# Later copies of the MLP's sums and a re-ordered head in a fused top-32 attention and MLP kernel

## The chip, the cores and the metric

The kernel runs on one core of a Trainium2 chip. The metric is the device time of one execution in microseconds, the median of several runs. Engines are called by their short names in the profile: PE (TensorE, matmuls; PEld its weight loads), DVE (VectorE), ACT (ScalarE), POOL (GpSimd) and SP (SyncE, which issues the DMAs).

## The reference

```python
scores = 1/sqrt(D) * q @ k^T                    # 8 batches, 8 heads, S=576, D=64
kth    = 32nd largest score of each row
attn   = softmax of the scores that are >= kth  # the others count as nothing
x      = (attn @ v), heads side by side         # 4608 x 512
h      = x @ w_in                               # 512 x 2048
g      = h where h >= 1, 0 where h <= -1, else (h + 1)^2 / 4
out    = g @ w_out                              # 2048 x 512
```

The two weight matrices arrive as 64-bit floats, which the kernel converts itself.

## The kernel before

**Work.** The attention is cut into 144 steps, called m: for each batch four tiles of 128 rows, each with four pairs of heads, and two more steps for the last 64 rows of each head. Each step goes through the engines:

- `scores` (L349): PE multiplies into `sp` (L367), ACT copies it to `s` (L368, two copies);
- the 32nd largest value on DVE: `more` and `less` are the larger and smaller of two halves of a row (L381, made for the step to come), then rounds of MAX8 and MATCH_REPLACE (L384 to L455) and a scan (L460);
- on ACT the negative maximum `nmax` (L402, it needs DVE's first `tops`, L401) and the exponentials `e` (L404);
- on DVE the masked sum (L467), which needs `e` and the 32nd value;
- division by the sum (`divide`, L411): in the head ACT makes a diagonal matrix `diag` (L417) and the division falls to the transpose on PE; later POOL divides (L420);
- the transpose of the weights: in the head by PE (`transpose_w` L476: `pw` L482, copies L485 and L489), later by DMA (`move_w` L493: ACT splits into `halves` L497, a DMA writes `rows`, a transposing DMA reads them into `wT`);
- `values` (L506): PE multiplies with v into `po` (L514, L522), ACT copies to `xT` (L527, L529).

When all four head pairs of a 128-row tile are done, `mlp` (L538) makes its work pending. There are 36 such chunks. A chunk has eight *hidden* blocks of 8 matmuls (PE, `ph`, L547), *reads* of each of them on ACT (`r` L558, `g` L566), *bounds* on POOL (L573, L575, L576) and 16 *final* matmuls into one PSUM tile `py` (L586). The profile counts each of these matmuls twice: 4608 for `ph` (36 x 64 x 2), so 16 a block and 32 finals a chunk. After the last of these ACT copies `py` into `y` (L589) and SP sends `y` out (L591). `py` has a single buffer, so the first final matmul of the next chunk waits for the copy. The last chunk is finished in halves (L600, L612).

**The head.** While the weights are converted (32 pieces of 512 words, `convert_piece` L141: `units` on ACT L147 and L148, `bits` on DVE L156, the addition on POOL L158), the steps m = 0 to 7 are *early*: four pieces a step, transposes by PE, one step of scores begun per step (slot 4). Step 8 is called `first_late` in the code: the first step after the last piece. Keys of the first batch are transposed by PE into `pk` and `pkt` (L261, L269) and copied to `kT` (L265, L274).

**What sets the order.** Every engine's order is written out by hand: all instructions are issued inside `manual_schedule`, in the order of the loop L801 to L890. A step has seven slots. In each slot the loop puts a part of the top-32 search, loads, transposes, values, scores and key preparation at fixed places; at its end `advance` hands out pending MLP work by a budget (`due`, a share of the work left), and `take` pops one item. `holding` keeps the reads of hidden blocks back in some slots, and `bounds` are delayed by two slots in late steps.

**Lines that the change touches.** `load_keys`/`keys_of` (copy engine at L264), `final` (L579 to L591), the start of the program (L779 to L785), the slot loop (L849 to L890). `LAG` is the number of hidden blocks that run ahead of the final matmuls.

Of the kernel before, what the change touches and what calls it, by code (L numbers as in the profile page):

```python
# [26 lines left out]
def kernel(  # L27
# [149 lines left out]
    def run(ctx, paired):  # L177
# [61 lines left out]
        def keys_of(b):  # L239

            kT = stage.tile([P, NHP, S], F32, name="kT")
            k_tl = stage.tile([TL, H, D], F32, name="k_tl", bufs=1)
            got = dict(kT=kT)

            def load_keys(hp):
                if b == 0:
                    k_in = xtp.tile([P, NK, P], F32, name="xT").rearrange("p c (j d) -> p c j d", j=2)
                else:
                    k_in = stage.tile([P, NT, 2, D], F32, name="k_in", bufs=1)
                for j in range(2):  # L250
                    nc.sync.dma_start(out=k_in[:, :, j, :], in_=whole(k, b)[:, 2 * hp + j])
                return k_in

            k_in = load_keys(0)
            nc.sync.dma_start(out=k_tl, in_=k[b, :, SM:S, :].rearrange("h p d -> p h d"))
            yield got
            for hp in range(NHP):
                k_next = load_keys(hp + 1) if hp + 1 < NHP and b == 0 else None
                pt = ps.tile([P, NT, P], F32, name="pk", tag="a", bufs=2)
                for c in range(NT):  # L260
                    nc.tensor.transpose(pt[:, c, :], k_in[:, c].rearrange("p j d -> p (j d)"), ident)  # L261
                for j in range(2):
                    d = slice(j * D, (j + 1) * D)
                    copy = nc.vector.tensor_copy if b == 0 and hp < 2 and j else nc.scalar.copy  # L264
                    copy(kT[d, hp, main(j)], pt[d].rearrange("p c n -> p (c n)"))  # L265
                if hp == 0:
                    pt = ps.tile([P, NHP, TL], F32, name="pkt", tag="a", bufs=2)
                    for h2 in range(NHP):
                        nc.tensor.transpose(pt[:, h2, :], k_tl[:, 2 * h2:2 * h2 + 2].rearrange("p j d -> p (j d)"),  # L269
                                            ident[0:TL, 0:TL])  # L270
                    for j in range(2):
                        d = slice(j * D, (j + 1) * D)
                        copy = nc.vector.tensor_copy if b == 0 and j else nc.scalar.copy
                        copy(kT[d, :, tail(j)], pt[d])  # L274
                k_in = load_keys(hp + 1) if hp + 1 < NHP and b else k_next
                if hp == NHP - 2:
                    loads = load_values(b)
                    got["v"], got["v_tl"] = next(loads)
                    for _ in loads:
                        pass  # L280
                yield got
# [256 lines left out]
        def mlp(xT, rows, pool, last):  # L538
# [39 lines left out]

            def final(f):  # L579
                if f == 0:  # L580
                    py.append(ps.tile([P, DM], F32, name="py", tag="py", bufs=1))
                if f // group not in gs:
                    issue_reads()
                while f // group not in whole_g:
                    bounds.popleft()[1]()
                nc.tensor.matmul(py[0], gs[f // group][:, f % group], w_out[:, f, :], start=(f == 0), stop=(f == NF - 1))  # L586
                if f == NF - 1:
                    y = (late or words).tile([P, DM], F32, name="y", bufs=1)
                    nc.scalar.activation(y, py[0], AF.Copy, scale=unit)  # L589
                    for p0, p1, dst in rows:  # L590
                        nc.sync.dma_start(out=dst, in_=y[p0:p1])  # L591

# [60 lines left out]
        total, spent = len(chunks) * (NK * NF + NF * DM // P), 0  # L655
        converted, inspected, due = 0, 0, 0.0

        reads, bounds, holding, slots_done = [], deque(), False, 0

        def issue_reads():  # L660
            while reads:
# [4 lines left out]
        def convert(time):  # L666

            nonlocal converted, begun
            while begun < min(converted + (2 if paired else 1), n_pieces):
                pipe.append(convert_piece(words, begun, not paired))  # L670
                next(pipe[-1])
                begun += 1
            next(pipe.popleft())
            converted += 1
            usable[converted] = time
            for i in range(begun, converted + (len(room) or 2)):
                load(words, i)
# [13 lines left out]
        def take():  # L691

            nonlocal spent, due, pe_time, taken
            cost, pieces, work, _ = pending[0]
            if pieces > converted or usable[pieces] > pe_time + 0.5:
                return False
            pending.popleft()
            due -= cost
            spent += cost
            pe_time += cost * UNIT_TIME  # L700
            work()
            taken = work.func
            return True
# [54 lines left out]
        def begin_at(m):  # L758
            nonlocal pe_time
            if m < n:  # L760
                queries(m)
                begin(m)
                pe_time += 1.15
                scored[m] = pe_time + 2.0
# [11 lines left out]
        issue(loads)  # L776
        convert(12.0)
        begin_at(0)
        convert(13.0)  # L779
        for _ in first_top(state[0]):  # L780
            pass
        begin_rest(state[0])
        for i in range(2):
            replace(state[0], 8, i)
        next(first)  # L785
        begin_at(1)
        next_keys, valued = 1, 0

        def values_until(m):
            nonlocal valued, pe_time  # L790
            while valued < min(m, n):
                pe_time = max(pe_time, ready_at[valued]) + 1.25
                values(state[valued])
                state[valued] = None
                if valued in ready:
                    ch = ready[valued]
                    mlp(xTs[ch], rows_of(*chunks[ch]), mlp_pool, ch == len(chunks) - 1)
                valued += 1

        first_late = None  # L800
        for m in range(n + 2):  # L801
# [3 lines left out]
            elif not early and late is None:  # L805
                conversion.close()
                room.clear()
                late = ctx.enter_context(tc.tile_pool(name="late", bufs=1))

            share, left = (total - spent) / (n + 2 - m), sum(x[0] for x in pending)  # L810
            for r in sorted(ready):
                if r + 4 > m and r >= valued:
# [11 lines left out]
            for slot in range(SLOTS):  # L824
# [24 lines left out]
                    judge(ps, att)  # L849
                if slot == 2 and (early or m == first_late or m >= n - 1):  # L850
                    values_until(m)
                if m == 0 and slot in (1, 2):
                    next(first)
                holding = not early and m % 2 == 0 and slot in (1, 2) and m < n
                if slot == 2 and not early:
                    if m % 2 == 0:
                        while len(reads) < 3 and pending and taken is not None and taken.__name__ == "hidden" and take():
                            pass
                    begin_until(min(m + 2, len(state)))
                    holding = False  # L860
                    issue_reads()
                    values_until((m - 2) // 2 * 2)
                    begin_until(m + 3 - m % 2)
                if slot == 4 and early:
                    begin_at(m + 2)
                if slot == (6 if early else 1):
                    queries(m + (3 if early else 5))
                    if (m < n and prep is None and next_keys < B and steps[m][0] == next_keys - 1 and steps[m][1] >= 1
                            and (next_keys > 1 or converted == n_pieces)):
                        prep = (turned_keys_of if next_keys > 1 else keys_of)(next_keys)  # L870
                    if prep is not None and (m % 2 == 0 or next_keys == 1):
                        got = next(prep, None)
                        pe_time += 0.5 if next_keys < 2 else 0.0
                        if got is None:
                            prep, next_keys = None, next_keys + 1
                        else:
                            keys[next_keys] = got
                            value_loads = got.get("loads", value_loads)
                    elif value_loads is not None:
                        loads.append(partial(next, value_loads, None))  # L880
# [3 lines left out]
                        nc.tensor.transpose(rest[:, i % NT, :], ident, ident)  # L884
                advance((EARLY_SHARE if early else share) / SLOTS if m < n - 2 else 32.0, now)
                slots_done += 1
                while bounds and (early or m >= n or bounds[0][0] < slots_done - 2):
                    bounds.popleft()[1]()
            for _ in (top_k if top_k is not None else ()):
                pass  # L890
        while pending:
            advance(32.0, pe_time + 8.0)
            while bounds:
                bounds.popleft()[1]()
        order.__exit__(None, None, None)


# [45 lines left out]
```

## Time and profile before

| what | value |
|---|---|
| median of 3 runs | 1471.31 us (1469.75 to 1472.52) |
| the profiled execution | 1471.88 us, of which the span is 1470.1 us |
| granted clock of PE in it, mean | 0.992 |
| busy: PE / DVE / ACT / POOL | 1433.2 / 1395.7 / 1160.2 / 930.9 us |
| DVE's waits for `s` (L381) | 8.8 us in 6 |
| DVE's waits for kT (L265) | 9.4 us in 2, one of them 8.0 at the start |
| PE's waits for `y` (L586) | 1.6 us in 1 |
| PE's waits for `wT` from the DMA (L514) | 4.1 us in 2 |

A line of the timeline reads: start and length in us, engine, line of the code, operation, what is written from what with shapes, how many instructions, and in brackets the idle time before it with the instruction that ended it. Lines of one kind that follow each other are put together (x2). A row of the table of stretches gives, for each engine, busy us and in brackets its instructions, then PE's granted clock (1.00 is full), the DMA engines' mean busy share and GB/s. All times are counted from the start of the span.

The kernel falls in two stages: the head with its conversion, up to about 150 us with its consequences to about 200 us, and a long regular middle in which a chunk takes 37.77 us (for example from the `y` at 1062.15 to that at 1099.92). The end after 1405 us is the rest of the last chunks' MLP.

### The profile page before, as it was taken

What the parts mean: (1) busy time and instruction counts of PE and PEld (TensorE: products, weight loads), DVE (VectorE), ACT (ScalarE), POOL (GpSimd) and SP (SyncE); (2) the same over time, 40 slices, a digit from 0 to 9 for tenths busy, and PEclk for the clock granted to TensorE, in tenths of its full rate; (3) what the DMA queues carried; (4) which work ended last, traced back from release to release, by engine and by line L of the source; (5) the groups of instructions that cost most, each with busy time, mean ns of one, the idle gap of its engine ahead of it and who ended that gap; (6) DMA issues with size and microseconds to landing.
All of it is one profiled execution on the core that took longest, in us unless ns stands there. A gap on an engine that the chain in (4) does not pass through costs nothing.

```text
span 1470.1 us, 32068 instructions
## 1 busy us (share of the span) xinstructions
PE 1433.2 (97%) x10787; PEld 1049.5 (71%) x10787; DVE 1395.7 (95%) x4392; ACT 1160.2 (79%) x2222; POOL 930.9 (63%) x1310
## 2 busy tenths in 40 slices
PE   6998899999999999999999999999999999999998
PEld 5776577777777777777777777777777777777777
DVE  6989999999999999999999999999999999999922
ACT  6986878888778888887778887888778888777642
POOL 3564577667666666666666666666666666666640
PEclk7999999999999999999999999999999999999999
DMA  7642766876778877886667797997667987665410
GB/s 233 199 133 57 201 161 183 217 188 165 164 177 211 217 200 192 210 218 177 173 168 204 207 216 177 224 215 181 174 165 187 224 214 175 167 163 151 137 41 17
DMA packets 508159, 260.42 MB, mean 177 GB/s; under 512 B 458704, under 2 KB 467152, under 8 KB 507984
## 3 DMA queue, kind: packets, MB, share of 16 engines
q1 hardware_dynamic: 507984, 258.27, 68.3%
q8 instruction: 87, 1.43, 0.4%
q14 instruction: 88, 0.72, 0.2%
HBM read 62.39 MB, written 102.63 MB: 112 GB/s over the span
## 4 chain that ended last, share of the span: by engine, by line
PE 91%; ACT 4%; DMA 2%; issue 1%; DVE 1%; SPq 1%; ACTq 0%
PE ph L547 34%; PE py L586 32%; PE sp L367 11%; PE po L514 10%; PE po L522 1%; PE pw L482 1%; DMA wT<-rows 1%; PE py_half L600 1%; ACT s L368 1%; ACT units L147 1%; ACT halves L497 1%; ACT wT L485 1%; ACT e L404 0%; DMA xT<-in_k_dram 0%; PE rest L884 0%
## 5 line engine op out<-in xcount | busy, mean ns | idle before, releaser
L547 PEld LDWEIGHTS ph<-xT,w_in 128*128 128x128 f32 x4608 | 547.0, 192 | 97.7 <-issue 66.8
L547 PE MATMUL ph<-xT,w_in 128*128 128x128 f32 x4608 | 555.6, 276 | 2.4 <-ACT g L566 1.8
L586 PE MATMUL py<-w_out,g 128*128 128x512 f32 x1120 | 526.6, 597 | 1.6 <-ACT y L589 1.6
L573 POOL TENSOR_SCALAR r<-r 128x256 f32<-128x256 f32 x280 | 138.3, 494 | 402.1 <-ACT r L558 397.9
L388 DVE MATCH_REPLACE8 more<-tops,more 128x288 f32<-128x288 f32 x864 | 379.1, 445 | 0.0
L420 POOL TENSOR_SCALAR e<-e,rz 128x576 f32<-128x576 f32 x268 | 304.3, 1145 | 12.6 <-DVE rz L413 12.6
L586 PEld LDWEIGHTS py<-w_out,g 128*128 128x128 f32 x1120 | 193.9, 191 | 164.9 <-issue 162.9
L497 ACT COPY halves<-e 128x1152 uint16<-128x1152 uint16 x268 | 293.8, 1144 | 0.0
L576 POOL TENSOR_TENSOR g<-r,g 128x256 f32<-128x256 f32 x280 | 233.4, 834 | 22.0
L467 DVE SCALAR_TENSOR_TENSOR e<-s,kth,e 128x577 f32<-128x577 f32 x288 | 242.9, 881 | 0.1
L404 ACT ACTIVATE e<-s,nmax 128x576 f32<-128x576 f32 x288 | 223.0, 775 | 4.7
L558 ACT ACTIVATE r<-ph,half 128x256 f32<-128x256 f32 (+1 forms) x296 | 136.9, 462 | 105.1 <-PE ph L547 100.5
L368 ACT ACTIVATE s<-sp 128x576 f32<-128x576 f32 x288 | 171.8, 650 | 43.2 <-PE sp L367 41.5
L575 POOL TENSOR_TENSOR r<-r 128x256 f32<-128x256 f32 x276 | 181.0, 656 | 23.0
L367 PE MATMUL sp<-kT,qT 64*128 64x288 f32 x1024 | 161.9, 434 | 4.8 <-ACT kT L265 3.4
L367 PEld LDWEIGHTS sp<-kT,qT 64*128 64x128 f32 x1024 | 89.8, 188 | 75.9 <-issue 30.5
L514 PE MATMUL po<-wT,v_in 128*64 128x128 f32 x2048 | 138.7, 276 | 4.9 <-DMA wT<-rows 4.1
L381 DVE TENSOR_TENSOR more<-s 128x576 f32<-128x576 f32 x144 | 134.7, 935 | 8.8 <-ACT s L368 8.8
L514 PEld LDWEIGHTS po<-wT,v_in 128*64 128x64 f32 x2048 | 113.4, 137 | 29.1 <-issue 12.2
L566 ACT ACTIVATE g<-ph,minus 128x256 f32<-128x256 f32 x280 | 130.8, 467 | 0.0
L429 DVE MAX8 tops<-more 128x8 f32<-128x288 f32 x288 | 125.9, 447 | 0.0
L437 DVE MAX8 tops<-more 128x8 f32<-128x288 f32 x288 | 117.0, 449 | 0.0
(95 smaller groups left out, 1370.1 us busy)
## 6 DMA issues: line engine op xcount, KB each, us to landing
rows<-halves SPq DMA_DIRECT2D x134, 576.0 KB, 3.2
lines<-parts SPq DMA_DIRECT2D x48, 256.0 KB, 3.3
q_in<-in_q_dram SPq DMA_DIRECT2D x32, 256.0 KB, 4.5
v_in<-in_v_dram SPq DMA_DIRECT2D x32, 256.0 KB, 4.0
raw<-in_moe_w_in_dram SPq DMA_DIRECT2D x32, 256.0 KB, 3.3
raw<-in_moe_w_out_dram SPq DMA_DIRECT2D x32, 256.0 KB, 3.2
out_dram<-y SPq DMA_DIRECT2D x31, 256.0 KB, 3.3
kT<-in_moe_w_in_dram SPq DMA_DIRECT2D x8, 512.0 KB, 4.5
```

The costliest lines, as they stand in the source:

```text
L367: nc.tensor.matmul(*x, start=True, stop=True)
L368: nc.scalar.activation(s[:, :, c0:c1], sp[:, :, 0:SH], AF.Copy, scale=SCALE)
L388: nc.vector.match_replace(out=st["rest"][:, i, :], in_to_replace=eight(st["tops"], i, r - 8), in_values=src[:, i, :], imm_value=LOWEST)
L404: nc.scalar.activation(e[:, i, :], s[:, i, :], AF.Exp, bias=nmax[:, i:i + 1])
L420: nc.gpsimd.tensor_scalar(st["e"][:, i, :], st["e"][:, i, :], rz[:, i:i + 1], 1.0, ALU.mult, ALU.mult)
L467: nc.vector.scalar_tensor_tensor(out=st["all"][1][:, i, :], in0=st["all"][0][:, i, :], scalar=last[i], in1=st["all"][1][:, i, :], op0=ALU. ...
L497: nc.scalar.copy(halves[:, :, i * S:(i + 1) * S], st["e"][:, i, :].bitcast(U16).rearrange("p (k t) -> p t k", t=2))
L514: nc.tensor.matmul(po[j * D:(j + 1) * D], v_in[:, h, c, :] if c < NT else tail_values(v_tl, h, t), wT[:, block(j, c)], start=(c == 0), sto ...
L547: nc.tensor.matmul(ph[:, i], w_in[:, kk, f * P:(f + 1) * P], xT[:, kk], start=(kk == 0), stop=(kk == NK - 1))
L575: nc.gpsimd.tensor_tensor(out=r, in0=r, in1=r, op=ALU.mult)
L576: nc.gpsimd.tensor_tensor(out=g, in0=r, in1=g, op=ALU.add)
L586: nc.tensor.matmul(py[0], gs[f // group][:, f % group], w_out[:, f, :], start=(f == 0), stop=(f == NF - 1))
```

## The change

Four edits; the computation is the same.

1. The copy of `py` into `y` and the output DMA are put into a queue, `outputs`. In the head (steps up to m = 8) an entry is issued more than three slots later, otherwise at the end of the slot of its last final matmul; the first final matmul of the next chunk always empties the queue first.
2. The second pair of keys is prepared right behind the first scores instead of after the first step's maxima; the second of its two copies goes from DVE to ACT.
3. Step 8 is treated like an early step for values, scores, queries and held reads: values first, then the scores of step 10, then up to `LAG` items of pending MLP work at once. The scores of step 11 and the next queries and keys come in step 9 instead.
4. The second batch's keys are prepared in odd late steps (9, 11, 13, 15) instead of in every step from 8 on; those of the later batches stay in even steps.

```diff
-                    copy = nc.vector.tensor_copy if b == 0 and hp < 2 and j else nc.scalar.copy
+                    copy = nc.vector.tensor_copy if b == 0 and hp == 0 and j else nc.scalar.copy
...
             def final(f):
                 if f == 0:
+                    while outputs:
+                        outputs.popleft()[1]()
                     py.append(ps.tile([P, DM], F32, name="py", tag="py", bufs=1))
...
                 if f == NF - 1:
-                    y = (late or words).tile([P, DM], F32, name="y", bufs=1)
-                    nc.scalar.activation(y, py[0], AF.Copy, scale=unit)
-                    for p0, p1, dst in rows:
-                        nc.sync.dma_start(out=dst, in_=y[p0:p1])
+                    outputs.append((slots_done, partial(give, py[0])))
+
+            def give(total):
+                y = (late or words).tile([P, DM], F32, name="y", bufs=1)
+                nc.scalar.activation(y, total, AF.Copy, scale=unit)
+                for p0, p1, dst in rows:
+                    nc.sync.dma_start(out=dst, in_=y[p0:p1])
...
         begin_at(0)
+        next(first)
         convert(13.0)
...
-        next(first)
         begin_at(1)
...
+            head = early or m == first_late
...
+                if slot == 2 and m == first_late:
+                    begin_at(m + 2)
+                    for _ in range(LAG):
+                        if pending:
+                            take()
...
-                holding = not early and m % 2 == 0 and slot in (1, 2) and m < n
-                if slot == 2 and not early:
+                holding = not head and m % 2 == 0 and slot in (1, 2) and m < n
+                if slot == 2 and not head:
...
-                if slot == (6 if early else 1):
-                    queries(m + (3 if early else 5))
+                if slot == (6 if head else 1):
+                    queries(m + (3 if head else 5))
...
-                    if prep is not None and (m % 2 == 0 or next_keys == 1):
+                    if prep is not None and (early or m % 2 == (1 if next_keys == 1 else 0)):
...
                 slots_done += 1
+                while outputs and (not head or outputs[0][0] < slots_done - 3):
+                    outputs.popleft()[1]()
...
             while bounds:
                 bounds.popleft()[1]()
+            while outputs:
+                outputs.popleft()[1]()
```

More of the change, by code (lines that the diff above doesn't have):

```diff
@@ L656, in run @@
         converted, inspected, due = 0, 0, 0.0
-        reads, bounds, holding, slots_done = [], deque(), False, 0
+        reads, bounds, outputs, holding, slots_done = [], deque(), deque(), False, 0
         def issue_reads():
```

## The prediction

> **What bounds the kernel now.** I read the page's engine totals first, then single stretches, because the totals mix two stages.
>
> ```profile
> PE 1433.2 (97%) x10787; PEld 1049.5 (71%) x10787; DVE 1395.7 (95%) x4392; ACT 1160.2 (79%) x2222; POOL 930.9 (63%) x1310
> ```
>
> TensorE and VectorE share the bound; ScalarE has room. The table of stretches says where (TensorE busy, weight loads, VectorE, ScalarE, GpSimd, clock, DMA share, GB/s).
>
> ```profile
> 118.00:137.00 19.00, 16.52 (x123) 1.00 0.23 62
> 137.00:165.00 28.00, 21.19 (x155) 0.94 0.61 175
> 165.00:196.00 31.00, 29.40 (x226) 1.00 0.63 165
> 256.00:1405.00 1149.00, 1148.90 (x8681) 1.00 0.75 189
> ```
>
> These rows count TensorE alone. From 256 to 1405 it never stands still, and VectorE doesn't either: both show 50.00 in every 50 us row. So nothing can be won there, only lost. Before 196 TensorE idles 2.48 + 6.81 + 1.60 = 10.9 us. There VectorE leads, and its waits are in its timeline (start, length, and in brackets the idle time before with its releaser).
>
> ```profile
> 16.98 0.69 DVE L265 COPY kT<-pk 64x512 f32<-64x512 f32 x1 [1.37 <-ACT kT L265]
> ...
> 131.55 0.76 DVE L381 TENSOR_TENSOR more<-s 128x576 f32<-128x576 f32 x1 [2.80 <-ACT s L368]
> ```
>
> ScalarE's timeline shows the old place of the sum's copy, `y`, first in the head, then at a chunk's end late in the kernel:
>
> ```profile
> 122.40 0.60 ACT L589 ACTIVATE y<-py 128x512 f32<-128x512 f32 x1 [2.91 <-PE py L586]
> 122.89 0.68 ACT L417 ACTIVATE diag<-ident,rz 128x128 f32<-128x128 f32 x2
> ...
> 1099.92 0.60 ACT L589 ACTIVATE y<-py 128x512 f32<-128x512 f32 x1 [0.88 <-PE py L586]
> 1100.72 0.21 ACT L402 ACTIVATE nmax<-tops 128x2 f32<-128x2 f32 x1 [0.20 <-DVE tops L401]
> ...
> 1102.81 2.19 ACT L497 COPY halves<-e 128x1152 uint16<-128x1152 uint16 x2
> 1104.90 0.77 ACT L404 ACTIVATE e<-s,nmax 128x576 f32<-128x576 f32 x1
> ```
>
> And TensorE's timeline shows who needs the one `py` buffer next:
>
> ```profile
> 195.39 1.10 PE L586 MATMUL py<-w_out,g 128*128 128x512 f32 x2 [1.60 <-ACT y L589]
> ```
> ```profile
> 1105.08 1.02 PE L586 MATMUL py<-w_out,g 128*128 128x512 f32 x2
> ```
>
> At 195 the copy already stood behind `halves` (194.65, ended 195.24), and TensorE waited. At 1105 it doesn't: `y` was over at 1100.52.
>
> [...]diag waits 2.91 us behind a `y` that it doesn't need. [...]The trace shows half (0.50) in 10.6–20.8, 24.2–31.05 and 143.7–147.1[...]. [...]`more` takes 0.74 us at best and 1.13 at 1098.15, where a division of GpSimd (L420) began at 1097.93.[...]
>
> **The change part by part.**
>
> *Second keys behind the first scores; one key copy moved to ScalarE.* VectorE loses the wait of 1.37 and the copy of 0.69 in step 0: 2.1 us. It could fall short: `sp` of step 1 at 17.00 had waited 3.40 for that kT, and s(1) was ready at 20.70 for a `more` at 21.19. Both kT copies now precede the second piece's units on ScalarE, and s(1) moves forward with them. The next key load is issued one weight load earlier on SP; behind it stands that weight load, one issue later. Price 0 to 2.1; I take −2.1.
>
> *Step 8 like the head.* The order of the engines in the changed program, timed with the durations of the same instructions before: without `y` ahead of diag, pw starts at 122.36 instead of 123.34, wT ends at 124.45, po runs 125.1–126.9, sp(10) follows at once, s(10) is ready at 128.85. So `more`(10) starts at about 128.9 and its 2.80 wait goes. What is late next: four hidden blocks now follow sp(10). 48 matmul records take 5.52 (L547 at 133.03), a block has 16, so 1.84, four 7.3: 128.0 to 135.3. Their four r/g pairs, then `y` (136.05), stand on ScalarE ahead of nmax(9) and e(9). The first half of e(9) is over at about 137.55, where the masked sum of step 9 (L467), come early, stands ready at 133.3: a new wait of 4.25. Net 4.25 − 2.80 = +1.43: step 9 ends at about 139.05 instead of 137.62. Behind it s(11) is ready at 141.9 for a need at 142.25, just in time. At 196 I take +1.2 of it as left (GpSimd's divisions move too). Bounds: −2.8 (no wait for e(9)) to +2.6[...].
>
> The sum for the head is −2.1 + 1.2 = −0.9, within ±1.2. It passes to the end, since TensorE's start at 195.39 hangs on ScalarE and so on VectorE.
>
> *Second batch's keys in odd steps.* Four pairs of kT copies (1.16) and pk (0.60) at steps 9 to 15 instead of 8 to 11, first used in step 18. Cover: two steps; without it one step's scores would come late. Price 0; up to 0.5 either way, since the copies stand before other r/g pairs.
>
> *Sums copied later.* In 23 chunks, those with `y` at 456.94 to 1288.94, `y` goes from ahead of nmax to behind both `halves`. (In the seven boundaries at 195 to 424 it stood there already; the last ones keep their place.) Of 0.60 us 0.49 is its own. Putting 0.49 behind the end of `halves`, and taking off `y` ahead of nmax where nmax didn't wait for VectorE (457, 609, 646), leaves against the next `py`: five boundaries with +0.12 to +0.38, and 18 short by 0.16 to 0.40, in sum 5.44. At 1105: halves end at 1105.00, plus 0.49 is 1105.49, `py` wanted 1105.08: short by 0.41. When TensorE does wait, it starts 0.15 after `y` ends (195.24 to 195.39): 18 × 0.15 = 2.7. Together 8.2 us, if every boundary pays in full.
>
> It does if VectorE, on whose tops nmax waits, falls back with TensorE; it pays once (0.6) if VectorE keeps its own pace and so arrives earlier at the next boundary. The trace has something between: the distance of `halves` to the next `py` leaves its level of about −0.23 or −0.37 three times by 0.5 to 0.6 (608.7, 948.8, 1288.9) and is back after one or two chunks. So a lead of VectorE costs it about as much per chunk as the lead is[...]. A lead d then meets wait w − d = d: half of w is paid, **4.1 us**. Bounds 0.6 and 8.2. The output DMA moves on SP to right ahead of the transposed reads (3.3 us landing); the read of w has 2 to 6 us of slack in odd steps: 0.
>
> *GpSimd's divisions one triple later*, once a chunk from 164 to 947. Example at 832.51: the triple can start when g is written (833.62), takes 0.40 + 0.61 + 0.73, the division then 1.47 to 2.77: over at 836.8 to 838.1; `halves` needs it at 838.10. Covered, barely. Bounds: `more` regains 0.23 there (hidden, as TensorE sets the pace), or `halves` slips 0.5 in 13 of these boundaries: 6.5. I take 0.
>
> Sum: the profiled execution has 1471.88 (span 1470.1 and 1.8 around it), 0.6 over the median of 1471.31. −0.9 + 4.1 = **+3.2**: 1475.1 against the profiled run, 1474.5 against the median. I give **1474.5**, own range 1472 to 1478.6.
>
> **Rivals.**
> 1. *Paid once.* VectorE runs on, ScalarE's chain comes 0.4 earlier, the wait vanishes: −0.9 + 0.6 gives 1471.0. For it: the slack in the boundaries 233 to 424, where `y` stands behind `halves` already, wanders between 0.33 and 1.88 with no second wait. Against it: from 495 on the distance is held.
> 2. *Faster: the hand-over of step 8 to 9 keeps both gains.* Place: the masked sum L467 of step 9. Price: −2.1 − 2.8 = −4.9, so 1466.4, if boundaries cost nothing. For it: TensorE has 10.9 us of idle time before 196 and the four blocks fill some. Against: r/g stand in strict order ahead of e(9). It decides at a wait for e(9) below 1.5 us, where the four blocks would have to end near 132.5.
> 3. *Full price.* VectorE follows TensorE entirely or `halves` slips behind the division: −0.9 + 8.2 gives 1478.6, more with a slip.
> That the change does nothing is excluded: copies and `y` do move in the built order.
>
> **How the numbers follow.** A difference under 0.2% (2.9 us) can't be told from none here. Forecast 0.48 (about 0.36 beyond that bound, 0.12 within), rival 1 0.18, rival 2 0.24, rival 3 0.10. Faster 0.24, same 0.12 + 0.18 = 0.30, slower 0.36 + 0.10 = 0.46. Range 1466.0 to 1479.5: from rival 2 to just over the full price.
>
> **What would show it.** Right: no copy L265 of keys on VectorE at 17; `more`(10) without its 2.80; a wait of about 4 us of L467 for e(9) near 133; TensorE's waits listing "py L586 <- ACT y" some 18 more times, 0.2 to 0.5 each, in sum 2 to 8 us; TensorE below 50.00 per 50 us after 457. Wrong: no such waits after 457 (rival 1), or L467 without wait (rival 2), or TensorE waiting in the middle for something that I gave nothing: wT or scores.

## The result, and the profile after

The changed kernel takes **1488.28 us** (median of 6, 1484.19 to 1489.44) against 1471.39 us (median of 6): ratio 1.0112, interval 1.0099 to 1.0126. It is slower, as forecast, but by 16.9 us where 3.2 were forecast, and outside the range. The profiled execution took 1486.83 us, with a span of 1485.0 us: 14.9 us more than the span before. Its page begins so:

```profile
PE 1442.5 (97%) x10787; PEld 1053.6 (71%) x10787; DVE 1410.0 (95%) x4391; ACT 1156.4 (78%) x2223; POOL 897.6 (60%) x1310
...
DVE 62%; PE 25%; ACT 5%; issue 5%; DMA 2%; SPq 0%; POOL 0%; ACTq 0%; POOLq 0%; DVEq 0%
```

The second line is the chain of work that ended last. Before, TensorE had 91% of that chain; now VectorE has 62%. VectorE has one instruction less than before and is busy 14.3 us longer. So the same instructions of VectorE have become longer.

TensorE in stretches of the changed kernel (columns as in the table of the prediction):

```profile
137.00:165.00 28.00, 23.56 (x146) 0.83 0.60 160
165.00:192.00 27.00, 26.28 (x213) 1.00 0.76 208
400.00:450.00 50.00, 49.59 (x366) 1.00 0.69 168
1050.00:1100.00 50.00, 49.78 (x343) 1.00 0.59 165
1350.00:1400.00 50.00, 50.00 (x345) 1.00 0.54 137
```

In the first row the granted clock is 0.83 where it was 0.94. In the middle TensorE now shows 0.2 to 0.4 us of idle time per 50 us row; behind the last chunk end with the new order it is full again. Its list of waits (who waits, for whom, total us, times, longest) begins:

```profile
PE py L588 <- ACT y L594: 7.1, 21, 0.8
PE po L514 <- DMA wT<-rows: 4.4, 4, 1.6
```

One wait for `y` before, 21 now, as the prediction had said. A chunk end in detail, first ScalarE, then TensorE, then VectorE and GpSimd a little later:

```profile
1076.14 2.19 ACT L497 COPY halves<-e 128x1152 uint16<-128x1152 uint16 x2
1078.24 0.58 ACT L594 ACTIVATE y<-py 128x512 f32<-128x512 f32 x1
1078.73 0.76 ACT L404 ACTIVATE e<-s,nmax 128x576 f32<-128x576 f32 x1
```
```profile
1073.22 5.52 PE L547 MATMUL ph<-xT,w_in 128*128 128x128 f32 x48
1078.97 1.10 PE L588 MATMUL py<-w_out,g 128*128 128x512 f32 x2 [0.22 <-ACT y L594]
1079.99 1.24 PE L367 MATMUL sp<-kT,qT 64*128 64x288 f32 x8
```
```profile
1085.47 0.84 DVE L467 SCALAR_TENSOR_TENSOR e<-s,kth,e 128x577 f32<-128x577 f32 x1
1086.25 0.08 DVE L467 DVE_READ_ACCUMULATOR e<-s,kth,e 128x1 f32 x1
1086.25 1.27 DVE L467 SCALAR_TENSOR_TENSOR e<-s,kth,e 128x577 f32<-128x577 f32 x1
```
```profile
1085.78 1.12 POOL L576 TENSOR_TENSOR g<-r,g 128x256 f32<-128x256 f32 x1
1086.88 0.90 POOL L573 TENSOR_SCALAR r<-r 128x256 f32<-128x256 f32 x1
```

`y` stands behind `halves`; the first final matmul waits for it, 0.22 us by the list. The add of GpSimd (L576) begins at 1085.78, while the first masked sum runs; it lasts 1.12 instead of 0.73, and the second masked sum, which comes due at 1086.25, takes 1.27. The same two masked sums before:

```profile
1112.35 0.89 DVE L467 SCALAR_TENSOR_TENSOR e<-s,kth,e 128x577 f32<-128x577 f32 x1
...
1113.17 0.94 DVE L467 SCALAR_TENSOR_TENSOR e<-s,kth,e 128x577 f32<-128x577 f32 x1
```

The 0.22 us are only a part of what is lost there, as the starts of the matmuls show. The same place of TensorE before, around the `py` at 1105.08 of the prediction:

```profile
1099.72 5.52 PE L547 MATMUL ph<-xT,w_in 128*128 128x128 f32 x48
1105.08 1.02 PE L586 MATMUL py<-w_out,g 128*128 128x512 f32 x2
1106.04 1.24 PE L367 MATMUL sp<-kT,qT 64*128 64x288 f32 x8
```

From the start of the hidden blocks to the first final matmul 5.36 us passed before and 5.75 pass now; from there to `sp` it was 0.96 and is 1.02. That makes 0.45 us a chunk, which is the difference between 38.23 and 37.77 but for rounding. Counted in this way over all chunks, from the first final matmul at 193 us to the one at 1308 (before 195 to 1294), TensorE loses 16.1 us: 11.3 at 20 waits for `y`, and nearly all of the rest behind `po`, where it waits for `wT` or `s` (4.3 us at 254, 600, 640 and 871 us by the list, before 0.5).

Start to start, summed over three chunks (before 1062 to 1175, after 1078 to 1193), VectorE's groups give:

| three chunks, us | before | after | difference |
|---|---|---|---|
| masked sums L467, 24 | 18.56 | 20.74 | +2.18 |
| `more`, 12 | 10.94 | 9.97 | -0.97 |
| all of VectorE | 113.31 | 114.70 | +1.39 |

VectorE never idles there, so these longer instructions are the chunk's length: 38.23 us instead of 37.77. (Between 732 and 848 us it is 38.40.)

Where the time lies follows from the start of each step's first masked sum, after less before: -3.72 us at step 8, -2.24 at step 9, -2.29 at step 15, then +15.4 on the way to step 132 (13.10), 13.30 at step 140; the last chunks' MLP adds the rest of the 14.9. The head won; the middle lost 0.53 us in each of some 29 chunks. Between steps 8 and 9 lies the new wait of VectorE for the exponentials:

```profile
133.76 1.01 DVE L467 SCALAR_TENSOR_TENSOR e<-s,kth,e 128x577 f32<-128x577 f32 x1 [4.28 <-ACT e L404]
```

Each kernel was profiled in one execution (number 5 in two), and heads differ between executions. At step 8 four profiled kernels of the experiments whose head up to there is that of before (2, 4, 12, 13) stand at -1.9 to +2.0 us against the execution before. So a few us of the head in one profile prove little.

### The profile page after: what moved, and what is told of

The parts are those of the page before. It is cut to its first block, busy times and chain, and to the rows that moved or that the text cites. A ratio compares the mean times of both kernels' runs of the same rounds, so it can differ in the third digit from the quotient of the medians.

```text
span 1485.0 us, 32095 instructions
## 1 busy us (share of the span) xinstructions
PE 1442.5 (97%) x10787; PEld 1053.6 (71%) x10787; DVE 1410.0 (95%) x4391; ACT 1156.4 (78%) x2223; POOL 897.6 (60%) x1310
## 3 DMA queue, kind: packets, MB, share of 16 engines
q8 instruction: 87, 1.43, 0.4%
## 4 chain that ended last, share of the span: by engine, by line
DVE 62%; PE 25%; ACT 5%; issue 5%; DMA 2%; SPq 0%; POOL 0%; ACTq 0%; POOLq 0%; DVEq 0%
DVE more L388 15%; DVE e L467 12%; PE ph L547 8%; PE py L588 8%; DVE less L381 6%; DVE more L381 5%; DVE tops L429 5%; DVE tops L437 5%; DVE tops L448 5%; DVE seconds L455 5%; DVE tops L401 3%; PE sp L367 3%; PE po L514 2%; PE pw L482 1%; DMA wT<-rows 1%
## 5 line engine op out<-in xcount | busy, mean ns | idle before, releaser
L388 DVE MATCH_REPLACE8 more<-tops,more 128x288 f32<-128x288 f32 x864 | 375.1, 437 | 0.0
L573 POOL TENSOR_SCALAR r<-r 128x256 f32<-128x256 f32 x280 | 134.9, 482 | 309.2 <-ACT r L558 305.0
L420 POOL TENSOR_SCALAR e<-e,rz 128x576 f32<-128x576 f32 x268 | 225.9, 853 | 156.1 <-DVE rz L413 156.1
L576 POOL TENSOR_TENSOR g<-r,g 128x256 f32<-128x256 f32 x280 | 280.2, 1001 | 22.0
L467 DVE SCALAR_TENSOR_TENSOR e<-s,kth,e 128x577 f32<-128x577 f32 x288 | 248.8, 899 | 4.4 <-ACT e L404 4.3
L575 POOL TENSOR_TENSOR r<-r 128x256 f32<-128x256 f32 x276 | 173.0, 627 | 23.0
L514 PE MATMUL po<-wT,v_in 128*64 128x128 f32 x2048 | 139.1, 276 | 5.5 <-DMA wT<-rows 4.4
L514 PEld LDWEIGHTS po<-wT,v_in 128*64 128x64 f32 x2048 | 113.6, 137 | 30.3 <-issue 9.0
L381 DVE TENSOR_TENSOR less<-s 128x576 f32<-128x576 f32 x144 | 129.8, 902 | 0.0
L429 DVE MAX8 tops<-more 128x8 f32<-128x288 f32 x288 | 125.4, 443 | 0.0
L381 DVE TENSOR_TENSOR more<-s 128x576 f32<-128x576 f32 x144 | 117.8, 818 | 5.2 <-ACT s L368 5.1
```

Of the source, the lines that this page charges most:

```text
L381: nc.vector.tensor_tensor(out=x, in0=s[:, :, 0:SH], in1=s[:, :, SH:S], op=op)
L388: nc.vector.match_replace(out=st["rest"][:, i, :], in_to_replace=eight(st["tops"], i, r - 8), in_values=src[:, i, :], imm_value=LOWEST)
L420: nc.gpsimd.tensor_scalar(st["e"][:, i, :], st["e"][:, i, :], rz[:, i:i + 1], 1.0, ALU.mult, ALU.mult)
L429: x()
L467: nc.vector.scalar_tensor_tensor(out=st["all"][1][:, i, :], in0=st["all"][0][:, i, :], scalar=last[i], in1=st["all"][1][:, i, :], op0=ALU. ...
L514: nc.tensor.matmul(po[j * D:(j + 1) * D], v_in[:, h, c, :] if c < NT else tail_values(v_tl, h, t), wT[:, block(j, c)], start=(c == 0), sto ...
```

## The experiments

Each is given with the kernel before on the same chip in the same hours, whose medians were 1472.3 to 1472.9 us. "Loss" and "gain" are against that. In the expectations the *built order* is the order of the instructions in the program as built, and *theory A* says that the place of the MLP's work against the steps makes the loss.

**1. The second keys alone.** The first two hunks of the change (copy engine, `next(first)` behind `begin_at(0)`), on the kernel before.

> The kernel before with the first part of the change alone: second keys behind the first scores, key copy on ScalarE. The order of the middle stays that of before. If this part carries the head's gain, step 8 comes about 3.7 us earlier, as in the changed kernel, and the time is 1466 to 1469 us. If the gain came from the other parts, or is eaten on the way to 195 us, it stays at 1471.

Measured 1470.45 us against 1472.88, ratio 0.9983 (0.9977 to 0.9990): a gain of 2.4 us, a little less than expected. In the profiled execution step 8 comes 2.93 us earlier, and 2.1 of it remain to the end. Over all profiled kernels, the eleven with this part stand at -1.9 to -3.7 us at step 8, -2.85 on average, and the five without it at 0.0 on average. So the gain of the head is real and lies mostly in this part. It is the fastest kernel of the study.

**2. Step 8 alone.** The hunks with `head`, the early scores and the `LAG` items.

> The kernel before with the step-8 part alone; the sum's copy is issued at once, as before. In the built order the last final matmul of a chunk, and so the copy y, nevertheless comes behind halves in nearly all chunks, and a division of GpSimd behind one more triple: four blocks taken early shift the planner's budget. Theory A (the place of the MLP work against the steps makes the loss): chunks of about 38.4 us, 1487 to 1491. Rival (the queue for the sums makes the loss): 1470 to 1474.

Measured 1485.19 us, ratio 1.0076 (1.0055 to 1.0098). No queue for sums is in this kernel; the loss is there. But the profiled execution, the slowest of the four (1491.39), isn't the picture that was expected. 6.9 us of its loss lie in the head (steps 1 to 14), its regular chunks take 37.77 and not 38.4, and TensorE doesn't wait for `y` in it at all, though `y` stands behind `halves`. So this run alone doesn't prove the middle.

**3. One more unit early.** On the changed kernel:

```diff
                     for _ in range(LAG):
                         if pending:
                             take()
+                    due += 4
```

> The changed kernel with the planner's budget raised by one final matmul (4 units) at step 8, nothing else. In the built order y then stands ahead of nmax in every chunk and GpSimd's order is that of before. Theory A: chunks of 37.77 us again, and the head's gain remains: 1467 to 1470. Rival (something else of the change, such as the later output transfers or the head's phase, slows the middle): 1483 to 1488.

Measured 1471.70 us, ratio 0.9995 (0.9984 to 1.0007). Some 16 us of loss are gone with one number of the planner. TensorE's row from 1050 to 1100 is full again:

```profile
1050.00:1100.00 50.00, 50.00 (x370) 1.00 0.59 168
```

Missed: the head's gain didn't remain. On TensorE it was gone in the head already: 1.5 us ahead at 180 us, it then waited 3.4 us for a load of queries (see number 6) and stood 2.2 us behind at 195. VectorE was still 2 us ahead at step 52, fell 3.8 us back between 543 and 700 us and stayed there.

**4. One unit less early.** The mirror, on the kernel before: `due -= 4` in slot 2 of the first late step.

> The kernel before with the planner's budget lowered by one final matmul (4 units) at step 8, nothing else. The built order then has y behind halves in 30 chunks and GpSimd's order of the changed kernel, with the old head. Theory A (place of the MLP work against the steps): 1482 to 1492. If the loss needs the changed head too: 1470 to 1474.

Measured 1490.98 us, ratio 1.0118 (1.0097 to 1.0139), with the old head. Its waits:

```profile
PE py L586 <- ACT y L589: 7.5, 20, 0.8
```

That is the loss of the changed kernel without any line of the change. The two runs together show what the step-8 part does to the middle: it takes four blocks early, the budget is then short, and the last final matmul of a chunk is handed out later, so that `y` stands behind `halves` at 30 chunk ends, 23 more than before.

**5. Last sum ahead of halves, the rest as changed.**

```diff
+                if slot == 3 and not head and pending and pending[0][2].func.__name__ == "final" and pending[0][2].args == (NF - 1,):
+                    take()
+                    while outputs:
+                        outputs.popleft()[1]()
```

> The changed kernel, but the last final matmul and y are put ahead of halves in each chunk; GpSimd's order stays that of the changed kernel. If the wait of the next sum for y (coupling TensorE to VectorE) is the cause, TensorE waits for nothing and the time is 1468 to 1472. If the division behind one more triple is the cause by itself[...], it stays at 1482 to 1488. Both halves come 0.5 us later here.

Inconclusive: of 13 executions three took 1473.5 to 1474.2 and ten 1481.5 to 1486.2 (median 1482.94, ratio 1.0061, 1.0045 to 1.0078). The profiled one was of the short group: chunks of 37.77, no wait for `y`. A second profile of the same kernel:

> The same kernel as sum_before_halves, for a profile of its slower executions (three of thirteen took 1474, the others 1481 to 1486). If GpSimd's order alone can hold VectorE in the slow distance, its chunks are 38.2 or more without any wait of TensorE for y; TensorE must then wait for something else, such as scores or wT.

Measured 1483.81. Chunks of 38.4, from 923 us on of 38.0, and TensorE's waits for others begin so:

```profile
PE po L514 <- DMA wT<-rows: 7.2, 3, 4.6
PE po L514 <- ACT g L566: 4.8, 16, 0.6
```

No `y`: here TensorE waits at `po` for a read `g` of ScalarE (16 times); `po` shares the three buffers of `ph`, which `g` empties. VectorE has 60% of the chain of work here, in the short execution under 1%. So `y` isn't the only instruction by which TensorE can be tied to VectorE, and the same program can settle in either pace.

**6. The change without step 8.** `head = early`, and without the early scores and items.

> The changed kernel without its step-8 part (no early blocks, step 8 as before); the second keys, the queue for sums and the odd steps stay. In the built order y and GpSimd's divisions stand as before from the eighth chunk end on. Theory A: the head gain of the second keys remains and nothing is lost: 1467 to 1471. If the queue or the odd steps cost the middle: 1480 or more.

Measured 1473.81 us, ratio 1.0004 (0.9992 to 1.0016): the middle isn't lost, so neither queue nor odd steps cost it. But the gain isn't there: VectorE was 5.5 us ahead at step 15, while TensorE, 3.2 us ahead at 180 us, was level at 195, and both were level with before at 700 us. TensorE waits for a load of queries:

```profile
184.60 0.63 PE L341 MATMUL pq<-ident,q_in 128*128 128x128 f32 x4 [2.65 <-DMA q_in<-in_q_dram]
```

SP issues that load at 180.16 here and at 177.10 before, though VectorE is ahead here. A wait for it at 182 to 187 us, 0.7 to 3.4 us long, stands in eight of the nine profiled kernels with the odd steps and in none of the seven without them. That points to the odd steps; no run changes them alone.

**7. y late, orders of TensorE and GpSimd kept.** On number 3: entries of the queue wait for slot 3.

```diff
-                while outputs and (not head or outputs[0][0] < slots_done - 3):
+                while outputs and (slot >= 3 if not head else outputs[0][0] < slots_done - 3):
```

> The kernel with one more unit early (1471.7), but the queue of sums is held until slot 3, so that y stands behind halves in every chunk while TensorE's and GpSimd's orders stay those of the fast version. If the place of y alone makes the loss: chunks of 38.2 or more with a wait of TensorE for y at most boundaries, 1482 to 1490. If GpSimd's order is needed as well: 1470 to 1476.

Measured 1486.21 us, ratio 1.0089 (1.0056 to 1.0121):

```profile
PE py L588 <- ACT y L594: 8.3, 17, 1.5
```

**8. The same, between the two copies of halves.** The queue is emptied inside the loop of `move_w`.

> As y_late_old_order (1486), TensorE's and GpSimd's orders untouched, but y is issued between the two copies of halves, 1.1 us earlier. If the wait of the next sum for y is what couples TensorE to VectorE, y is now out of the way by 0.6 us or more: no waits for y in the regular chunks, 37.77 us each, 1470 to 1475. If any place of y behind the first nmax costs as much, 1483 to 1488.

Measured 1479.71 us, ratio 1.0046 (1.0025 to 1.0066): between the two. Missed: the waits didn't go. They became short, too short for the list: start to start, the first final matmul comes 0.33 us behind the last hidden one instead of 0.11. Once a chunk another 0.15 go in the same way at `po`. Chunks still take 38.2. ScalarE, then TensorE:

```profile
1070.49 1.14 ACT L497 COPY halves<-e 128x1152 uint16<-128x1152 uint16 x1
1071.53 0.59 ACT L596 ACTIVATE y<-py 128x512 f32<-128x512 f32 x1
1072.02 1.14 ACT L497 COPY halves<-e 128x1152 uint16<-128x1152 uint16 x1
```
```profile
1072.27 1.10 PE L590 MATMUL py<-w_out,g 128*128 128x512 f32 x2
```

TensorE starts 0.15 after the end of `y`, just as when `y` came 1.1 us later. It runs up to where `y` stands in both kernels.

**9. The same, one slot later still** (`slot >= 4`), behind the second exponential and a read pair.

> As y_late_old_order (1486), but y is issued one slot later still, behind the second exponential and a read pair (some 1.4 us later). If each chunk end pays what y is late (the prediction's sum), 30 ends pay 1.4 us more: about 1525. If the wait only fixes at which distance TensorE follows VectorE, and VectorE's own pace at that distance sets the chunk, the dose does not add: 1480 to 1495, chunks of 38 to 38.6, TensorE's waits for y still under 1 us per chunk.

Measured 1496.67 us, ratio 1.0168 (1.0141 to 1.0195). 10.5 us over number 7, not the 42 of 30 x 1.4; regular chunks take 38.0, less than in number 7, and the excess lies in single chunks of 39 to 41.6 us and at the end. Missed in part: six waits for `y` are long enough for the list, up to 3.1 us. The lateness of `y` isn't paid once per chunk. That the place of `y` sets the distance of the two engines, and the distance VectorE's pace, fits this.

**10. The change without the add on GpSimd.** L576 is left out, so g lacks the quadratic part.

> The changed kernel without the add of the bound on GpSimd (g keeps only its linear part, so the output is another). If VectorE sets the pace[...], VectorE gains 0.5 to 1 us a chunk, TensorE's waits for y go and chunks take 37.77: 1467 to 1472. If the waits for y hang on ScalarE's order alone, whatever GpSimd does: 1480 to 1488.

Measured 1478.37 us, ratio 1.0038 (1.0028 to 1.0047), and apart from 1.2 us at the very end no wait of TensorE for `y` is listed; most chunks take 37.77. `y` is where it was. So GpSimd's adds are needed for most of the loss. Whether by the longer instructions of VectorE where the two engines meet (1.27 instead of 0.80 us for a masked sum) or by the time that the adds take on GpSimd isn't separated: without them GpSimd is busy 671.5 us instead of 897.6, and TensorE runs at another distance, where `y` is over in time. Missed in size: single chunks of 38.6 to 40.4 remain, in some of which VectorE now waits for ScalarE (`more` 8.8 us, masked sums 7.5 us in all).

**11. Second keys and queue.** Number 1 with the queue, without step 8 and odd steps.

> The kernel before with the second keys behind the first scores and the queue for sums (which in the built order only moves y behind diag at step 8), without step 8's early blocks and without odd steps. The middle's order is that of before. If the diag that no longer waits for y adds to the gain of the keys: 1466 to 1470, below only_second_keys. If VectorE's gain there does not reach TensorE: 1470 to 1472.

Measured 1472.33 us, ratio 0.9997 (0.9985 to 1.0008). The freed diag adds nothing at the end. VectorE's lead at step 8 was 1.9 us in the profiled execution, and TensorE had 0.8 of it at 195 us and nothing at 700.

**12. The kernel before with y late.** Queue with `slot >= 3`; every instruction of TensorE and GpSimd stands as before, and only `y` moves, in the chunks from 457 us on.

> The kernel before, with the one change that y is issued behind halves in every chunk from 457 us on; TensorE's and GpSimd's orders and the whole head are exactly those of before. If y's place alone makes the loss: TensorE waits for y at most chunk ends, chunks of 38.2 to 38.4, 1482 to 1488. If the loss needs the moved division or the new head: 1470 to 1474.

Measured 1484.43 us, ratio 1.0077 (1.0057 to 1.0096). The place of `y` alone makes a loss of 11.6 us. How it does so this trace doesn't show: the profiled execution was the fastest of the four (1480.93, the others 1484.3 to 1485.3), and TensorE's waits for `y` are only 0.4 us in 2 in it. It ran in chunks of 38.2 to 40.0, but for one, from 424 to 655 us, with waits for `wT` (6.9 us in 4 at L514, before 4.1 in 2). Then it fell into chunks of 37.77 with `y` in the same place, nearly all of them: TensorE had dropped so far behind VectorE that `y` was over in time. A trace with the waits for `y` in the old order is that of number 7.

**13. A copy behind halves for which nobody waits.** On the kernel before, `y` in its old place, and in each chunk

```diff
                     move_w(state[m - 1])
+                    if given and late is not None:
+                        given.clear()
+                        spare = late.tile([P, DM], BF16, name="spare", bufs=1)
+                        nc.scalar.activation(spare, w_out[:, 0, :], AF.Copy, scale=unit)
```

> The kernel before with a copy more on ScalarE behind halves in each chunk (a 128x512 read of w_out into a spare tile[...]), for which nobody waits; y stays ahead of nmax. If the loss comes from the 0.5 us that ScalarE's later work (e, r, g and so GpSimd) slips against VectorE: chunks of 38.2 or more, 1482 to 1488. If it comes from the tie of TensorE to y: 37.77, no waits for y, 1470 to 1475.

Measured 1477.99 us, ratio 1.0030 (1.0019 to 1.0041): between the two answers. TensorE's row is full in one stretch and not in a later one:

```profile
800.00:850.00 50.00, 50.00 (x382) 1.00 0.85 216
1100.00:1150.00 50.00, 49.60 (x353) 1.00 0.73 190
```

From 1028 us on chunks take 38.24, and TensorE waits 0.4 at a `po` for a `g` of ScalarE. 2.8 us of this execution's loss stand there at 198 us already, in a head that is that of before; 4.1 come after 1028. So work on ScalarE at this place makes 5 us without `y`, by the medians, and again with a wait of TensorE for ScalarE. Whether the 11.6 us of number 12 contain these 5 isn't shown.

**What they show together.** Distance from the start of a step's first masked sum on VectorE to the first final matmul of a chunk on TensorE, in regular chunks. The nearest masked sum is taken; where the distance is negative, the final matmul comes first. "At `y`" means that TensorE starts 0.15 us behind the end of `y`, so that it is held there.

| kernel | distance, us | chunk, us |
|---|---|---|
| before; one more early (late part) | 2.10 to 2.25 | 37.77 |
| changed; y late, old order | 2.64, at `y` | 38.23 to 38.40; 38.38 |
| y between halves | 1.59, at `y` | 38.21 |
| copy behind halves, up to 880; from 1028 | 3.68; 1.39 | 37.77; 38.24 |
| sum before halves, short; long execution | -2.56 to -3.2; 1.2 to 1.6 | 37.77; 38.4, later 38.0 |
| before with y late, from 655 | -3.2 | 37.77 |
| y behind e | -3.1, at `y` | 38.01 |

A chunk takes 37.77 where TensorE's rows show 50.00, no idle time. The reading that fits these rows is this; it is put together from them, and no run sets the distance alone. Where VectorE would need more than that at some distance, since its instructions are longer where they meet GpSimd's (a masked sum 1.27 instead of 0.80), TensorE and with it GpSimd's bounds creep forward against VectorE, until either the two meet otherwise and VectorE needs 37.77 too (before: distance 2.10), or TensorE runs into an instruction of ScalarE that stands behind VectorE's tops (changed: `y`, at 2.64). Then the distance is held where VectorE is slow, and VectorE sets the chunk. The distance alone doesn't decide, since orders differ too: 2.10 is a good one in one order, 1.59 and 2.64 are bad in others, and some -3 gives 37.77 or 38.01.

## Why the prediction was wrong, point by point

- **What bounds the kernel: half right.** Both engines without idle time was seen. "So nothing can be won there, only lost" held. That equality was read as VectorE being held to TensorE's pace; what VectorE would need at another distance was in the trace before, in the chunks from 232 to 424 (38.2 on average, without idle time of VectorE), and not priced.
- **Second keys: right, if anything too small.** -2.1 taken; -3.7 at step 8 in the changed kernel, -2.93 by itself and -2.85 on average (experiment 1).
- **Step 8: right.** A wait of L467 of 4.25 predicted, 4.28 measured; +1.43 predicted, +1.48 measured from step 8 to step 9. What was left of the head at 196 was -2.3 instead of -0.9, within the spread of heads. The upper bound of +2.6 was an estimate. Between 120 and 200 us TensorE's granted clock was at half (0.50) from 136.1 to 139.5 and from 146.3 to 153.2, before only from 143.7 to 147.1; what that cost isn't separated.
- **Odd steps: taken at 0; nothing seen in the middle, but probably a cost in the head** (experiment 6): the wait for queries near 185 us, 0.7 to 3.4 us where the bound was 0.5. It is 0.7 in the changed kernel's profile. That part was never run alone.
- **"Sums copied later": the step that failed, with its term "half of w is paid".** Three things in it. First the cause: the queue doesn't move `y` in the middle; the step-8 part does, by the budget (experiments 3, 4, 6). Second the term itself, 4.1 us with bounds 0.6 and 8.2. It lets VectorE gain a lead that takes half off each wait. VectorE gained none: it never idles, its own instructions became longer, and the wait doesn't shrink from chunk to chunk (0.22 or 0.23 us in the list at each of the seven ends from 964 to 1194). In the 23 chunks of the forecast 18 waits are listed, as many as were forecast, but they were paid whole: start to start they cost 10.0 us (0.50 to 0.83 instead of 0.11 from the last hidden to the first final matmul, and 0.08 in the next pair). VectorE lost 12.3 us there (steps 40 to 132). That the sum "paid in full", 8.2, comes near to this is in part luck, since the lateness of `y` doesn't set the size of the wait (experiment 9). VectorE's pace at the held distance does, less TensorE's own: 38.2 to 38.4 less 37.77, with the single longer chunks 0.53 on average. Third the count: the seven chunk ends from 195 to 424, where `y` already stood behind `halves`, were taken as unchanged; VectorE lost 3.1 us there (-2.29 at step 15, +0.81 at step 40) as divisions and finals moved. 12.3 and 3.1 make the 15.4 us of the middle.
- **GpSimd's divisions: taken at 0, not settled by itself.** They aren't needed for the loss (experiments 7 and 12). With them in the new order the sum before halves still loses in ten of thirteen executions (experiment 5), and experiment 4 loses 0.4% more than 12; the intervals just miss each other.
- **Rival 3 (full price)** was nearest: "VectorE follows TensorE entirely". It was the other way about: TensorE follows VectorE.
- **What would show it wrong** named waits in the middle for `wT` or scores. Three of some size are new (at 600, 640 and 871 us, 3.0 us in all), the smaller part of the miss; its plain sign was the chain of work, which moved from TensorE to VectorE.

**Left open.** How the loss splits between the slip of ScalarE's work and the tie of TensorE to `y`: experiments 12 and 13 lose 11.6 and 5.1 us, in executions that change pace on the way, and a difference of the two isn't a measured share. What makes one execution settle in the short pace and another in the long one. And why the lead of VectorE after the head reaches the end in experiment 1 but not in 6 and 11; for 6 the wait for queries is one reason.

## What to carry to other kernels

When two engines run without idle time at the same pace, ask what each would need alone at another distance from the other; a new dependence between them is priced by the slower pace at which it holds them (here 38.23 us a chunk instead of 37.77), not by the waits that it shows (0.22). A budget in a planner is part of the program: compare the built orders far from the edit, and find out which edit moved what, before giving a price. A copy that empties a single buffer belongs ahead of the instructions that wait for the other engine: `y` behind `halves` cost 11.6 us in experiment 12. And take the cost of a wait of TensorE from the starts of its matmuls: the list showed 0.22 us where 0.45 were lost.

## What was not expected of the hardware

- One program has more than one steady pace: 37.77 or 38.4 us a chunk in executions of the same kernel (experiment 5), and changes from one to the other within an execution (experiments 12 and 13), at unchanged orders and a mean granted clock of 0.990 to 0.993 in the profiled executions.
- Where instructions of VectorE and GpSimd meet for more than 0.05 us, the one that begins while the other runs is mostly the longer for it. From 200 to 1390 us, masked sums that met none of GpSimd's took 0.80 to 0.83 us (142 before, 157 after), those that began while one ran 0.81 to 1.28 (109 and 82). GpSimd's adds that met no masked sum, `more` or `less` took 0.72 to 0.74 (99 and 117), those that began while one ran 1.12 to 2.02 (32 and 111). Single ones: the masked sum 1.27 instead of 0.80, the add of GpSimd 1.12 or 1.91 (at 1081.12) instead of 0.73, a division pair 2.56 (at 1108.02 before) or 1.47 (at 1083.01 after). With the change GpSimd's divisions became shorter (1145 to 853 ns on average) and its adds longer (834 to 1001).
